# Attention in a fused kernel: reciprocals widened on GpSimd and transposed, last scores in two equal halves, first k loads from ACT's queue, a new table of places

## Chip, cores and metric

The kernel runs on one core of a Trainium2 chip. The metric is the device time of one execution in microseconds. The engines are called PE (TensorE matmul; PEld is its weight load), DVE (VectorE), ACT (ScalarE), POOL (GpSimd) and SP (SyncE, which here issues most DMAs).

## The reference

Three layers follow one another. The change is in the first one alone.

```
# q, k, v: (4 batches, 8 heads, 576 positions, 64), float32
scores = scale * np.matmul(q, k.transpose(0, 1, 3, 2))
mask = block_i >= block_j                    # blocks of 64 positions
scores = np.where(mask, scores, -1000000000.0)
scores = scores - np.max(scores, axis=-1, keepdims=True)
attn = np.exp(scores)
attn = attn / (np.sum(attn, axis=-1, keepdims=True) + 1e-09)
x = np.matmul(attn, v)                       # -> (2304 tokens, 512)
...
h = x @ w_in                                 # 512 -> 2048
g = np.maximum(h, 0.0) + np.log1p(np.exp(-np.abs(h)))
x = g @ w_out                                # 2048 -> 512
...
# routed layer: 8 experts of 512 -> 1024 -> 512, for tokens with x @ w_skip > 0
```

## The kernel before

**Attention.** The 32 heads are worked on in 16 pairs of heads. A pair's 576 queries are four tiles of 128 (t = 0 to 3) and a last one, t = 4 (TAIL), which holds the last 64 queries of both heads side by side in 128 rows. For each pair the kernel runs these steps. In brackets stand the engine and the function; a step's digits are tile and head, so TP40 is step TP of tile 4.

- T (PE, `transposes_qk`): transposes q (T0), k (T1) and the last rows of both (T2); T3 is the first 128 rows of pair 0. H (ACT, `split_high`) and L (DVE, `split_low`) split the result into a high and a low part.
- S (PE, `scores`): the scores of tiles 0 and 1, 2, 3 and 4, three products each (high x high, high x low, low x high). M (DVE, `maxima`) and E (ACT, `exps`): maxima, exponentials and their sums into `sm`.
- TP (PE, `transposes_p`) and EV (ACT or DVE, `evacuate_p`): transposed probabilities, brought out of PSUM. TP40 ends with a fifth transpose (L440) into the bank `v`, which EV5 (DVE) evacuates.
- V (PE, `values`): V00 for the first 256 queries, V10 for the rest.
- R (DVE, `reciprocals`): the nine sums of each row become reciprocals, and each is written as a high and a low part into `rr`. RT (PE, L490) transposes `rr`; RK (ACT, L494) copies the result to `rT`; RM (PE, L501 and L503) multiplies `rT` with the constant `spread`, so that each row of 64 outputs gets its query's reciprocal. RX (ACT) brings that out of PSUM, and N0, N1 (DVE) multiply the values with it.
- C (POOL, DVE, ACT): one piece of the weights of w_in and w_out is converted beside each pair. ldqk, ldv and ldp (SP) load the rows of a later pair and a later piece.

**What sets the order.** Each engine works its instructions off in program order. The steps of neighbouring pairs are mixed: `WHEN` gives each step a place in units of a pair, `SHIFT` corrects it for pairs 0, 1, 2, 14 and 15, and `in_order` emits, of the steps whose needs and buffers are met, the one with the lowest place:

```
step:      steps_of[key] = Step(do, needs, p + WHEN[name] + SHIFT.get((p, name), 0.0))
in_order:  if best is not None and s.when >= best.when:
               continue
```

The tiles in PSUM that T, TP and RM write come from a pool of two (`tp`), so each such step waits for the evacuation of an earlier one. The scores have two buffers (`s`).

**Start and end.** Before the steps, SP issues the loads of pairs 0 and 1 in order (`load_first`, `load_pair`), and PE runs 15 matmuls whose result nobody reads (`keep_busy`). With the last pair's steps are mixed the first splits of x and of weights (L546 to L557) and the first matmuls with w_in (`layer1`, L568, called layer 1 below; `layer2`, L620, called layer 2, multiplies with w_out).

Of the kernel before, what the change touches and what calls it, by code (L numbers as in the profile page):

```python
# [9 lines left out]
F32 = mybir.dt.float32  # L10
# [12 lines left out]
def attention_softplus_moe_kernel(  # L23
# [133 lines left out]
    def load_pair(p, names="qkv", first=0):  # L157

        b, hp = divmod(p, NP)
        for nm in names:  # L160
            src = {"q": q, "k": k, "v": v}[nm]
            t = ld[p, nm] if first else (v_p if nm == "v" else qk_p).tile([P, TT, 2, D], F32, tag=nm, name=nm + "r")
            full = S // P
            for h in range(2):
                nc.sync.dma_start(
                    out=t[:, first:full, h, :],
                    in_=src[b, 2 * hp + h, first * P:full * P, :].rearrange("(t p) d -> p t d", p=P),
                )
            if nm == "q":
                for h in range(2):  # L170
                    r = slice(h * D, (h + 1) * D)
                    nc.sync.dma_start(out=q_last[p % 2][r, r], in_=src[b, 2 * hp + h, full * P:S, :])
            else:
                nc.sync.dma_start(
                    out=t[:, full, :, :], in_=src[b, 2 * hp:2 * hp + 2, S - P:S, :].rearrange("h p d -> p h d")
                )
            ld[p, nm] = t

    def load_first():
        for nm, src in (("q", q), ("k", k)):  # L180
            t = ld[0, nm] = qk_p.tile([P, TT, 2, D], F32, tag=nm, name=nm + "r")
            nc.sync.dma_start(out=t[:, 0, :, :], in_=src[0, 0:2, 0:P, :].rearrange("h p d -> p h d"))
# [104 lines left out]

    NR = 2 * FULL + 1
    spread = pt_p.tile([P, TT + 1, P], F32R, tag="spread", name="spread")
    rrs = [pt_p.tile([P, P], F32R, tag=f"rr{i}", name=f"rr{i}") for i in range(2)]  # L290
# [72 lines left out]
    def scores(p, t):  # L363
# [26 lines left out]
    def maxima(p, t):  # L390

        ps, mx = sc_ps[p, t]
        if t == TAIL:
            nc.vector.tensor_reduce(
                out=mx[:, 0:1], in_=ps.rearrange("p h n -> p (h n)")[:, 0:S], axis=AX.X, op=ALU.max, negate=True
# [91 lines left out]
    rs = {}  # L487
# [676 lines left out]
    nc.scalar.preload_act_table_set("natural_log_exp_and_others")  # L1164
# [3 lines left out]
    load_pair(0, "qk", 1)  # L1168
    load_pair(1, "qk")
# [4 lines left out]
    nc.vector.memset(ones, 1.0)  # L1174
# [13 lines left out]

    def setup_spread():
        for t in range(TT):  # L1190
            for h in range(2):
                c = 2 * t + (h if t < TAIL else 0)
                a, b = (ident[:, x:x + 1].to_broadcast([P, D]) for x in (c, NR + c))
                nc.gpsimd.tensor_tensor(
                    out=spread[:, t + h if t == TAIL else t, h * D:(h + 1) * D], in0=a, in1=b, op=ALU.add
                )
# [6 lines left out]
    class Step:  # L1203
# [20 lines left out]
        "Cc": 0.783, "Cd": 0.485, "Ce": -4.674, "ldp": 1.12, "ldqk": -8.02, "ldv": -4.508, "spread": 0.656,  # L1224
        "setup": 9.277, "load_routing": -1.996, "move": 0.847, "x00": 0.917, "x10": 0.463, "x01": -0.61, "x11": -1.972,
        "x02": -0.686, "x12": -4.773, "x03": -0.39, "x13": 2.078, "wi0": -5.142, "wi1": -0.474, "wi2": 1.753,
        "l10": 3.513, "l11": 15.15, "sp": 16.397,
# [470 lines left out]
```

## Time and profile before

| | us |
|---|---|
| median of 3 runs | 721.88 (721.18 to 723.02) |
| the profiled execution | 721.51 |
| its span | 719.8 |
| PE busy | 688.5 (96%) |
| DVE busy | 473.8 (66%) |
| ACT busy | 369.1 (51%) |
| POOL busy | 155.8 (22%) |

The times of the trace count from the span's start. The shares of the whole span mix the stages; a stage is read by itself from the table of windows. A matmul's row overlaps the next one's, so the time that PE needs for one is read from the distance of two starts. The idle time in front of an instruction is put down to what ended it. The granted clock of 0.989 is a mean over the span.

### The profile page before, as it was taken

To read this page: it belongs to the slowest core of one execution; us is meant where nothing else is said; L and a number is where in the kernel's file an instruction comes from. 1 tells how busy PE (TensorE), PEld (TensorE's weight loads), DVE (VectorE), ACT (ScalarE), POOL (GpSimd) and SP (SyncE) were. 2 spreads that over 40 slices of the span, in tenths; PEclk is the share of its full clock that TensorE was granted. 3 is DMA by queue.
4 is the path that set the end of the run, shared out by engine and by line. 5 is a ranking of instruction groups with operands and counts; after the bars stand their busy time and mean duration, and the time that the engine had idled before them with its cause. 6 is when DMAs were issued, how large, how long until landed. Compare 5 with 4: busy or idle time off the path is not lost. (4 is left out here: it accounts for less than half of the span.)

```text
span 719.8 us, 11563 instructions
## 1 busy us (share of the span) xinstructions
PE 688.5 (96%) x4184; PEld 534.6 (74%) x4184; DVE 473.8 (66%) x983; ACT 369.1 (51%) x884; POOL 155.8 (22%) x177
## 2 busy tenths in 40 slices
PE   6999999999979999999999999999999999987996
PEld 5767777777757888888888888888888777776742
DVE  4677777868786985668665688767665355564322
ACT  3877887878776655465444454444453232320111
POOL 1311112121244543112211122112110021113120
PEclk9999999999999999999999999999999999998999
DMA  6534435542210011011101011100002030984620
GB/s 155 133 85 95 109 89 108 123 115 69 52 59 30 31 58 30 30 59 60 30 29 59 29 48 41 58 30 31 0 1 86 32 118 11 337 303 165 225 76 11
DMA packets 88740, 57.80 MB, mean 80 GB/s; under 512 B 67391, under 2 KB 76607, under 8 KB 88674
## 3 DMA queue, kind: packets, MB, share of 16 engines
q1 hardware_dynamic: 87378, 54.73, 26.1%
q0 software_dynamic: 1296, 2.24, 1.0%
q8 instruction: 35, 0.57, 0.3%
q14 instruction: 31, 0.25, 0.1%
HBM read 46.16 MB, written 10.92 MB: 79 GB/s over the span
## 5 line engine op out<-in xcount | busy, mean ns | idle before, releaser
L568 PE MATMUL h<-xs,wi 128*128 128x512 f32 (+1 forms) x960 | 217.4, 376 | 0.0
L568 PEld LDWEIGHTS h<-xs,wi 128*128 128x128 f32 x960 | 170.5, 191 | 35.9 <-issue 0.9
L620 PE MATMUL o<-wo,gh 128*128 128x512 f32 x576 | 182.6, 398 | 0.0
L620 PEld LDWEIGHTS o<-wo,gh 128*128 128x128 f32 x576 | 106.3, 188 | 23.3
L267 POOL TENSOR_TENSOR cc<-cc,cb 128x512 f32<-128x512 f32 (+1 forms) x40 | 43.5, 1087 | 355.9 <-DVE cb L265 164.6
L583 DVE SCALAR_TENSOR_TENSOR e<-h,e 128x512 f32<-128x512 f32 (+1 forms) x80 | 50.8, 635 | 104.7 <-ACT e L581 104.2
L620 PE MATMUL o<-wo,gl 128*128 128x512 f32 x288 | 114.1, 396 | 0.0
L579 ACT ACTIVATE e<-h 128x512 f32<-128x512 f32 (+1 forms) x80 | 44.1, 551 | 134.3 <-PE h L568 134.3
L409 ACT ACTIVATE p<-s,mx 128x128 f32<-128x128 f32 (+2 forms) x144 | 78.4, 552 | 8.1 <-DVE mx L399 5.7
L589 DVE TENSOR_TENSOR gl<-e,gh 128x512 fp32r<-128x512 f32 (+1 forms) x80 | 65.4, 818 | 6.5
L399 DVE TENSOR_REDUCE mx<-s 128x2 f32<-128x256 f32 (+1 forms) x64 | 52.5, 822 | 19.0 <-PE s L388 9.8
L620 PEld LDWEIGHTS o<-wo,gl 128*128 128x128 f32 x288 | 54.2, 188 | 13.2
L437 PE MATMUL tp<-ident,p 128*128 128x128 f32 x384 | 59.6, 285 | 2.7 <-DMA vr<-in_v_dram 1.0
L463 ACT ACTIVATE pt<-tp 128x512 f32<-128x512 f32 (+1 forms) x80 | 43.8, 553 | 30.9 <-PE tp L437 30.6
L481 PE MATMUL v<-pt,vr 128*64 128x320 f32 (+4 forms) x448 | 50.3, 364 | 0.0
L581 ACT ACTIVATE e<-e 128x512 f32<-128x512 f32 (+1 forms) x80 | 47.2, 590 | 2.5
L580 ACT ACTIVATE e<-e 128x512 f32<-128x512 f32 (+1 forms) x80 | 47.2, 590 | 2.6
L588 DVE CAST gh<-e 128x512 fp32r<-128x512 f32 (+1 forms) x80 | 43.8, 547 | 6.4
L437 PEld LDWEIGHTS tp<-ident,p 128*128 128x128 f32 x384 | 41.8, 142 | 5.9 <-issue 1.3
L751 POOL DMA_INDIRECT lst<-pay,si x18 | 17.7, 984 | 126.8 <-DVE pay L744 83.2
L481 PEld LDWEIGHTS v<-pt,vr 128*64 128x64 f32 x448 | 29.3, 136 | 18.4 <-issue 2.7
L259 ACT ACTIVATE cc<-raw 128x512 f32<-128x512 uint32 (+1 forms) x40 | 22.9, 573 | 24.3 <-POOL ca L268 24.3
(249 smaller groups left out, 945.2 us busy)
## 6 DMA issues: line engine op xcount, KB each, us to landing
xs<-in_moe_w_dram SPq DMA_DIRECT2D x16, 512.0 KB, 8.2
raw<-in_moe_w_in_dram SPq DMA_DIRECT2D x12, 512.0 KB, 3.7
raw<-in_moe_w_out_dram SPq DMA_DIRECT2D x12, 512.0 KB, 3.2
xd<-xT SPq DMA_DIRECT2D x18, 256.0 KB, 4.0
out_dram<-xT SPq DMA_DIRECT2D x18, 256.0 KB, 4.1
vr<-in_v_dram SPq DMA_DIRECT2D x32, 128.0 KB, 2.5
qr<-in_q_dram SPq DMA_DIRECT2D x30, 128.0 KB, 2.8
kr<-in_k_dram SPq DMA_DIRECT2D x30, 128.0 KB, 2.7
```

The lines of the kernel that those rows point to most:

```text
L399: nc.vector.tensor_reduce(out=mx[:, c:c + 2], in_=ps[:, :, columns(t)], axis=AX.X, op=ALU.max, negate=True)
L409: nc.scalar.activation(out=pn[t, h], in_=x, func=AF.Exp, bias=mx[:, c:c + 1], accum_out=sums[p][:, 0, 2 * t + h:2 * t + h + 1])
L437: nc.tensor.transpose(ps[:, at:at + P], pn[t, g][:, j * P:(j + 1) * P], ident)
L463: nc.scalar.activation(out=dst, in_=x, func=AF.Copy)
L481: nc.tensor.matmul(out=ps[h * D:(h + 1) * D, c0 - q0:q1 - q0], lhsT=vt[:, kt, h, :], rhs=rhs, start=(kt == 0), stop=(kt == nk - 1), skip_g ...
L568: nc.tensor.matmul(out=ps[:, 0:n], lhsT=a[:, kc, :], rhs=b[:, 0:n], start=(kc == 0 and j == 0), stop=(kc == KC - 1 and j == 2),)
L579: nc.scalar.activation(out=e[:, 0:n], in_=ps[:, 0:n], func=AF.Abs)
L580: nc.scalar.activation(out=e[:, 0:n], in_=e[:, 0:n], func=AF.Exp, scale=-1.0)
L581: nc.scalar.activation(out=e[:, 0:n], in_=e[:, 0:n], func=AF.Ln, bias=1.0)
L583: nc.vector.scalar_tensor_tensor(out=g[:, 0:n], in0=ps[:, 0:n], scalar=0.0, in1=e[:, 0:n], op0=ALU.max, op1=ALU.add)
L589: nc.vector.tensor_tensor(out=gl[:, 0:n], in0=g[:, 0:n], in1=gh[:, 0:n].bitcast(F32), op=ALU.subtract)
L620: nc.tensor.matmul(out=acc[c, t], lhsT=a[:, ts], rhs=b, start=(fc == f0 and j == 0), stop=(fc == f1 - 1 and j == 2),)
```

## The change

- Reciprocals: `rr`, `rT` and `spread` go, with RT, RK and the two operations that made high and low parts. A new step RB (POOL, L493) copies eight of the nine reciprocals of each row 64 times, to `rb` (128x512). RM becomes five transposes (L502, L504): four of `rb`, and one of the ninth reciprocal, broadcast to 128 columns, into the bank `v`. RX evacuates the last 64 queries in two halves of 64 rows. RM now also needs EV5.
- The last scores are two groups of three matmuls of 288 columns each, in place of 512 and 64.
- The first loads of k (four DMAs) are issued from ACT's queue, ahead of its table load. Six such matmuls of `keep_busy` (idle matmuls, below) are put before each of T0 and T1 of pair 0.
- The table of places is new throughout; the set-up of the routed layer moves to the start.

```
-            for k0, n in ((0, FULL * P), (FULL * P, REM)):
+            n = S // 2
+            for g in range(2):
                 for j, (x, y) in enumerate(((bh, kh), (bh, kl), (bl, kh))):
                     nc.tensor.matmul(
-                        out=ps[:, int(k0 > 0), 0:n], lhsT=x, rhs=y[:, k0:k0 + n],
-                        start=(j == 0), stop=(j == 2),
+                        out=ps[:, g, 0:n], lhsT=x, rhs=y[:, g * n:(g + 1) * n], start=(j == 0), stop=(j == 2),
                     )
...
     def reciprocals(p):
 
-        sm = sums.pop(p)
-        t = rrs[p % 2]
+        sm = sums[p]
         nc.vector.tensor_scalar(out=sm[:, 1, :], in0=sm[:, 0, :], scalar1=1e-9, scalar2=None, op0=ALU.add)
         nc.vector.reciprocal(out=sm[:, 0, :], in_=sm[:, 1, :])
-        nc.vector.tensor_copy(out=t[:, 0:NR], in_=sm[:, 0, :])
-        nc.vector.tensor_tensor(out=t[:, NR:2 * NR], in0=sm[:, 0, :], in1=t[:, 0:NR].bitcast(F32), op=ALU.subtract)
...
-    def rows_of_reciprocals(p):
-        nc.tensor.transpose(pv[p, 0][:, HALF:HALF + P], rrs[p % 2].bitcast(F32), ident)
-
-    def keep_rows(p):
-        rs[p] = st_p.tile([P, P], F32R, tag="rT", name="rT", bufs=2)
-        nc.scalar.activation(out=rs[p], in_=pv[p, 0][:, HALF:HALF + P], func=AF.Copy)
+    def widen_reciprocals(p):
+
+        r = sums[p][:, 0, 0:2 * FULL]
+        rbs[p] = pt_p.tile([P, 2 * FULL, D], F32, tag="rb", name="rb")
+        nc.gpsimd.tensor_copy(
+            out=rbs[p], in_=r.rearrange("p (c o) -> p c o", o=1).to_broadcast([P, 2 * FULL, D])
+        )
 
     def spread_reciprocals(p):
 
         ps = pts[p, "r"] = ps_t.tile([P, 512], F32, tag="tp", name="tp")
-        r = rs.pop(p)
+        rb = rbs.pop(p).rearrange("p c d -> p (c d)")
         for t in range(FULL):
-            nc.tensor.matmul(out=ps[:, t * P:(t + 1) * P], lhsT=spread[:, t, :], rhs=r, start=True, stop=True)
-        for h in range(2):
-            nc.tensor.matmul(
-                out=pv[p, 0][:, HALF:HALF + REM], lhsT=spread[:, TAIL + h, :], rhs=r[:, h * REM:(h + 1) * REM],
-                start=(h == 0), stop=(h == 1), skip_group_check=True,
-            )
+            nc.tensor.transpose(ps[:, t * P:(t + 1) * P], rb[:, t * P:(t + 1) * P], ident)
+        r = sums.pop(p)[:, 0, NR - 1:NR]
+        nc.tensor.transpose(pv[p, 0][:, HALF:HALF + P], r.to_broadcast([P, P]), ident)
...
+            queue = nc.scalar if (nm, first) == ("k", 1) else nc.sync
...
+        if p == 0 and part < 2:
+            keep_busy(6)
...
     WHEN = {
-        "T3": -1.506, "H3": -4.329, "L3": -3.148, "T0": -0.851, "H0": -5.283, "L0": -4.901, "T1": -0.314,
+        "T3": -1.826, "H3": -30.966, "L3": -27.97, "T0": -0.797, "H0": -29.404, "L0": -27.87, "T1": -0.348,
...
-        add("RT", (), rows_of_reciprocals, [k("R"), k("V", 0, 0)], args=())
-        add("RK", (), keep_rows, [k("RT")], args=())
-        add("RM", (), spread_reciprocals, [k("RK"), k("V", 0, 0)], args=())
-        ring("rr", 2, k("R"), [k("RT")])
+        add("RB", (), widen_reciprocals, [k("R")], args=())
+        ring("rb", 1, k("RB"), [k("RM")])
+        ring("sm", 2, k("S", 0), [k("RM")])
+        add("RM", (), spread_reciprocals, [k("RB"), k("EV5"), k("V", 0, 0)], args=())
```

**The order on PE, a pair in the middle, before.** From step T2 (`q_last` and the last rows `kr`) to the second half of the values (`v<-pt`, 64x320). `p_144` is the probabilities of the last tile, `rr_139` the packed reciprocals. Rows that only repeat the one above are left out, here and in the fences below.

```order
L316 MATMUL tp<-ident,q_last_123 128x128 [waits DMAHW5_49,DMAHW4_49,DVE_49]
L316 MATMUL tp<-ident,kr 128x128 [waits DMAHW0_49]
L490 MATMUL v<-ident,rr_139 128x128
L437 MATMUL tp<-ident,p_144 128x128 [waits Activation_49]
L440 MATMUL v<-ident,p_144 128x128 [waits Activation_49]
L384 MATMUL s<-k0h,q0h 128x512 x2
...
L312 MATMUL tp<-ident,kr 128x128 [waits DMAHW7_49,DMAHW6_49,Activation_49]
L501 MATMUL tp<-rT,spread 128x128 [waits DVE_49]
L503 MATMUL v<-rT,spread 128x64 [waits DVE_49]
L481 MATMUL v<-pt_912,vr 64x320 x6
```

The transpose of the reciprocals (L490) stands ahead of step TP40, whose last transpose (L440) writes the same bank `v` and waits for ACT.

The same place after the change, from V00 (64x256) on; `p_141` is now the last tile's probabilities, `p_138` those of tile 3.

```order
L481 MATMUL v<-pt_912,vr 64x256 [waits DMAHW1_49]
L437 MATMUL tp<-ident,p_141 128x128 [waits Activation_49]
L440 MATMUL v<-ident,p_141 128x128
L384 MATMUL s<-k0h,q0h 128x384 x2
...
L316 MATMUL tp<-ident,q_last_123 128x128 [waits DMAHW5_49,DMAHW4_49,DVE_49]
L437 MATMUL tp<-ident,p_138 128x128 [waits Activation_49]
L384 MATMUL s<-k0h,q0h 128x512 [waits Activation_49]
L502 MATMUL tp<-ident,rb 128x128 [waits Activation_49,Pool_49]
L504 MATMUL v<-ident,sm 128x128 [waits DVE_49]
L312 MATMUL tp<-ident,kr 128x128 [waits DMAHW7_49,DMAHW6_49,DVE_49]
L481 MATMUL v<-pt_904,vr 64x320 x6
```

TP40 with L440 has moved ahead of the 384-column scores and of T2; the reciprocals are transposed after the 512-column scores and before T1, and wait for POOL there.

**The order on PE at the end of attention, before.** From the last pair's V00 to the first products of layer 1 (`h<-xs,wi`); `p_144` is the last tile's probabilities.

```order
L481 MATMUL v<-pt_3056,vr 64x128 x2
L437 MATMUL tp<-ident,p_141 128x128 [waits Activation_49]
L437 MATMUL tp<-ident,p_142 128x128 [waits Activation_49]
L490 MATMUL v<-ident,rr_139 128x128 [waits DVE_49]
L437 MATMUL tp<-ident,p_144 128x128 [waits Activation_49]
L440 MATMUL v<-ident,p_144 128x128 [waits Activation_49]
L501 MATMUL tp<-rT,spread 128x128 [waits PE_49]
L568 MATMUL h<-xs,wi 128x512 x2
...
L481 MATMUL v<-pt_3154,vr 64x320 [waits Activation_49]
```

The same place after the change.

```order
L481 MATMUL v<-pt_3035,vr 64x128 x2
L437 MATMUL tp<-ident,p_141 128x128 [waits Activation_49]
L440 MATMUL v<-ident,p_141 128x128
L437 MATMUL tp<-ident,p_138 128x128 [waits Activation_49]
L437 MATMUL tp<-ident,p_139 128x128 [waits Activation_49]
L502 MATMUL tp<-ident,rb 128x128 [waits Activation_49,Pool_49]
L504 MATMUL v<-ident,sm 128x128 [waits DVE_49]
L481 MATMUL v<-pt_3103,vr 64x320
L570 MATMUL h<-xs,wi 128x512 [waits Activation_49]
```

L490 is gone, TP40 has moved to the front, and the last values, which stood behind the first product of layer 1, now stand ahead of it.

**The order on POOL, one pair in the middle, after the change.** `ca`, `cc` and `wi` are the weight conversion's tiles.

```order
L251 TENSOR_TENSOR ca<-raw 128x256 [waits DMAHW4_49,Pool_49]
L493 COPY rb<-sm 128x512 [waits DVE_49,PE_49,Activation_49]
L268 TENSOR_TENSOR cc<-cc,cb 128x256 [waits DVE_49]
L269 TENSOR_TENSOR wi<-ca,cc 128x256 [waits Pool_49]
L251 TENSOR_TENSOR ca<-raw 128x256 [waits DMAHW4_49,Pool_49]
```

The copy is new; it stands between the first and the last part of a piece's conversion.

## Rows read from the trace of the kernel before

**Rows 1.** Table of stages: us, busy us (instructions) per engine, granted clock, DMA share, GB/s.

```profile
0.00:8.57 8.57, 4.59 (x25) 3.31 (x26) 1.49 (x6) 2.54 (x5) 2.87 (x16) 1.00 0.46 105
8.57:22.04 13.47, 11.54 (x63) 9.29 (x62) 8.86 (x18) 7.18 (x26) 2.72 (x6) 1.00 0.81 189
22.04:47.82 25.78, 24.20 (x215) 18.51 (x214) 18.83 (x44) 20.11 (x63) 5.41 (x14) 1.00 0.43 103
47.82:197.51 149.69, 147.52 (x1298) 112.53 (x1297) 115.14 (x278) 119.67 (x372) 26.48 (x45) 1.00 0.40 95
197.51:229.02 31.51, 26.61 (x183) 20.27 (x182) 22.05 (x41) 21.16 (x52) 13.52 (x11) 0.95 0.14 42
229.02:555.00 325.98, 325.98 (x1474) 266.55 (x1473) 231.72 (x367) 162.93 (x288) 78.32 (x60) 1.00 0.11 37
```

**Rows 2.** PE in order of time, one pair: start, us, instruction, count.

```profile
74.69 0.44 PE L384 MATMUL s<-k1h,q1h 64*128 64x384 f32 x2
74.98 0.34 PE L384 MATMUL s<-k1l,q1h 64*128 64x384 f32 x2
75.15 0.34 PE L384 MATMUL s<-k1h,q1l 64*128 64x384 f32 x2
...
76.93 0.33 PE L316 MATMUL tp<-ident,q_last 128*128 128x128 f32 x1
...
77.21 0.27 PE L490 MATMUL v<-ident,rr 128*128 128x128 f32 x1
77.31 0.60 PE L437 MATMUL tp<-ident,p 128*128 128x128 f32 x4
78.06 0.33 PE L440 MATMUL v<-ident,p 128*128 128x128 f32 x1
...
79.12 0.20 PE L388 MATMUL s<-ones,unseen 64*128 64x64 bf16 x2
...
80.43 2.28 PE L481 MATMUL v<-pt,vr 128*64 128x320 f32 x20
...
83.16 0.47 PE L373 MATMUL s<-k1h,bd1h 128*128 128x512 f32 x1
...
84.18 1.09 PE L437 MATMUL tp<-ident,p 128*128 128x128 f32 x8
85.20 0.33 PE L384 MATMUL s<-k0h,q0h 64*128 64x128 f32 x2
```

**Rows 3.** PE's weight loads, the same pair: who waited for whom, us, times, longest.

```profile
PEld v L440 <- ACT rT L494: 0.4, 1, 0.4
PEld tp L316 <- DVE q0l L340: 0.3, 1, 0.3
```

**Rows 4.** The start in order of time, all engines.

```profile
0.82 1.28 ACT L1164 ACT_TABLE_LOAD   x1 [0.82 <-PEq L1682]
...
4.12 1.12 SPq L165 DMA_DIRECT2D kr<-in_k_dram  x2
...
4.72 0.87 PE L312 MATMUL tp<-ident,qr 128*128 128x128 f32 x3 [0.46 <-DMA qr<-in_q_dram]
...
7.34 0.88 PE L312 MATMUL tp<-ident,kr 128*128 128x128 f32 x3 [1.75 <-DMA kr<-in_k_dram]
...
18.71 1.06 PE L437 MATMUL tp<-ident,p 128*128 128x128 f32 x4
```

**Rows 5.** PE's longest waits from 197.51 to 218 us.

```profile
PE v L490 <- DVE rr L420: 3.2, 1, 3.2
PE v L490 <- DVE pt L466: 1.1, 1, 1.1
```

**Rows 6.** PE in order of time, the first products of layer 1.

```profile
217.15 4.03 PE L568 MATMUL h<-xs,wi 128*128 128x512 f32 x12
...
223.31 5.86 PE L568 MATMUL h<-xs,wi 128*128 128x512 f32 x24
```

**Rows 7.** POOL's groups of instructions by form: busy us, mean ns, idle before.

```profile
L549 POOL TENSOR_TENSOR xs<-xT,xs 128x512 fp32r<-128x512 f32 x10 | 14.4, 1446 | 12.6 <-ACT xs L546 10.6 <-DVE xs L548 2.0
```

More of the change, by code (lines that the diff above doesn't have):

```diff
@@ L164, in load_pair @@
             for h in range(2):
-                nc.sync.dma_start(
+                queue.dma_start(
                     out=t[:, first:full, h, :],
@@ L171, in load_pair @@
                     r = slice(h * D, (h + 1) * D)
-                    nc.sync.dma_start(out=q_last[p % 2][r, r], in_=src[b, 2 * hp + h, full * P:S, :])
+                    queue.dma_start(out=q_last[p % 2][r, r], in_=src[b, 2 * hp + h, full * P:S, :])
             else:
-                nc.sync.dma_start(
+                queue.dma_start(
                     out=t[:, full, :, :], in_=src[b, 2 * hp:2 * hp + 2, S - P:S, :].rearrange("h p d -> p h d")
@@ L179, in load_first @@
     def load_first():
-        for nm, src in (("q", q), ("k", k)):
+        for nm, src, queue in (("q", q, nc.sync), ("k", k, nc.scalar)):
             t = ld[0, nm] = qk_p.tile([P, TT, 2, D], F32, tag=nm, name=nm + "r")
-            nc.sync.dma_start(out=t[:, 0, :, :], in_=src[0, 0:2, 0:P, :].rearrange("h p d -> p h d"))
+            queue.dma_start(out=t[:, 0, :, :], in_=src[0, 0:2, 0:P, :].rearrange("h p d -> p h d"))
     w_in_i = w_in.bitcast(I32)
@@ L288, in attention_softplus_moe_kernel @@
     NR = 2 * FULL + 1
-    spread = pt_p.tile([P, TT + 1, P], F32R, tag="spread", name="spread")
-    rrs = [pt_p.tile([P, P], F32R, tag=f"rr{i}", name=f"rr{i}") for i in range(2)]
     pt2 = pt_p.tile([P, 2, REM], F32, tag="pt2", name="pt2")
@@ L394, in maxima @@
             nc.vector.tensor_reduce(
-                out=mx[:, 0:1], in_=ps.rearrange("p h n -> p (h n)")[:, 0:S], axis=AX.X, op=ALU.max, negate=True
+                out=mx[:, 0:1], in_=ps[:, :, 0:S // 2], axis=AX.XY, op=ALU.max, negate=True
             )
@@ L406, in exps @@
             sums[p] = st_p.tile([P, 2, NR], F32, tag="sm", name="sm", bufs=2)
-        x = ps.rearrange("p h n -> p (h n)")[:, 0:S] if t == TAIL else ps[:, h, columns(t)]
+        if t == TAIL:
+            x, y = ps[:, :, 0:S // 2], pn[t, h].rearrange("p (g n) -> p g n", g=2)
+        else:
+            x, y = ps[:, h, columns(t)], pn[t, h]
         c = 2 * int(t == 1) + h
         nc.scalar.activation(
-            out=pn[t, h], in_=x, func=AF.Exp, bias=mx[:, c:c + 1], accum_out=sums[p][:, 0, 2 * t + h:2 * t + h + 1]
+            out=y, in_=x, func=AF.Exp, bias=mx[:, c:c + 1], accum_out=sums[p][:, 0, 2 * t + h:2 * t + h + 1]
         )
     def reciprocals(p):
-        sm = sums.pop(p)
-        t = rrs[p % 2]
+        sm = sums[p]
         nc.vector.tensor_scalar(out=sm[:, 1, :], in0=sm[:, 0, :], scalar1=1e-9, scalar2=None, op0=ALU.add)
         nc.vector.reciprocal(out=sm[:, 0, :], in_=sm[:, 1, :])
-        nc.vector.tensor_copy(out=t[:, 0:NR], in_=sm[:, 0, :])
-        nc.vector.tensor_tensor(out=t[:, NR:2 * NR], in0=sm[:, 0, :], in1=t[:, 0:NR].bitcast(F32), op=ALU.subtract)
     PT = {}
@@ L485, in values @@
                 )
[L487 to L494 removed]
+    rbs = {}
+    def widen_reciprocals(p):
[4 more added lines that the diff above has]
+        )
     def spread_reciprocals(p):
         ps = pts[p, "r"] = ps_t.tile([P, 512], F32, tag="tp", name="tp")
[L499 removed]
+        rb = rbs.pop(p).rearrange("p c d -> p (c d)")
         for t in range(FULL):
[L501 to L506 removed]
+            nc.tensor.transpose(ps[:, t * P:(t + 1) * P], rb[:, t * P:(t + 1) * P], ident)
+        r = sums.pop(p)[:, 0, NR - 1:NR]
+        nc.tensor.transpose(pv[p, 0][:, HALF:HALF + P], r.to_broadcast([P, P]), ident)
     def x_of(p, q0, q1):
@@ L514, in keep_reciprocals @@
         nc.scalar.activation(out=x_of(p, 0, FULL * P), in_=pts.pop((p, "r")), func=AF.Copy)
-        nc.scalar.activation(out=x_of(p, FULL * P, S), in_=pv[p, 0][:, HALF:HALF + REM], func=AF.Copy)
+        for h in range(2):
+            r = slice(h * D, (h + 1) * D)
+            nc.scalar.activation(
+                out=x_of(p, FULL * P, S)[r], in_=pv[p, 0][r, HALF + h * REM:HALF + (h + 1) * REM], func=AF.Copy
+            )
     def normalise(p, half):
@@ L1163, in attention_softplus_moe_kernel @@
     ctx.enter_context(tc.manual_schedule())
-    nc.scalar.preload_act_table_set("natural_log_exp_and_others")
+    nc.vector.memset(ones, 1.0)
     for i in range(2):
@@ L1168, in attention_softplus_moe_kernel @@
     load_pair(0, "qk", 1)
+    nc.scalar.preload_act_table_set("natural_log_exp_and_others")
     load_pair(1, "qk")
@@ L1173, in attention_softplus_moe_kernel @@
     load_pair(1, "v")
-    nc.vector.memset(ones, 1.0)
     keep_busy(15)
@@ L1179, in attention_softplus_moe_kernel @@
         nc.gpsimd.memset(unseen[h * D:h * D + 1, 0:BLK], UNSEEN)
-    for i in range(2):
-        nc.gpsimd.memset(rrs[i].bitcast(F32), 0.0)
     nc.gpsimd.memset(pt2[0:P - REM], 0.0)
-    nc.gpsimd.memset(spread.bitcast(F32), 0.0)
     nc.gpsimd.memset(zeros, 0.0)
@@ L1187, in attention_softplus_moe_kernel @@
     nc.gpsimd.memset(blank[:, :, :, 1], 0)
[L1189 to L1196, printed above, removed]
     X0 = "avvpavvp"
@@ L1215, in attention_softplus_moe_kernel @@
     WHEN = {
[8 rows of a table removed]
[L1224 to L1227, printed above, removed]
[8 rows of a table added]
+        "Cd": 1.473, "Ce": -0.906, "ldp": 0.848, "ldqk": -26.137, "ldv": 0.17, "setup": -0.563, "load_routing": 5.725,
+        "move": -0.595, "x00": 1.495, "x10": 2.034, "x01": -3.314, "x11": 0.114, "x02": 0.457, "x12": 1.475,
+        "x03": 0.222, "x13": -0.717, "wi0": 0.166, "wi1": -26.631, "wi2": 1.078, "l10": 6.37, "l11": 7.064,
+        "sp": 0.291,
     }
     SHIFT = {
[40 rows of a table removed]
-        (0, "setup"): -0.494, (0, "load_routing"): -0.944, (15, "move"): -0.122, (15, "x00"): 0.015, (15, "x01"): -0.8,
-        (15, "x02"): -0.002, (15, "x12"): -0.023, (15, "x03"): -0.172, (15, "x13"): -0.299, (15, "wi0"): -0.377,
-        (15, "wi1"): 0.868, (15, "wi2"): 0.077, (15, "l10"): 1.051, (15, "l11"): -0.144, (15, "sp"): -1.119,
[28 rows of a table added]
+        (2, "Ce"): -0.385, (2, "ldp"): 0.487, (15, "ldqk"): 0.167, (15, "ldv"): 0.687, (15, "L0"): 0.288,
[8 rows of a table added]
+        (15, "Cd"): -2.47, (15, "Ce"): 0.189, (15, "ldp"): 1.597, (0, "setup"): 0.607, (0, "load_routing"): -1.46,
[3 rows of a table added]
     }
@@ L1417, in attention_softplus_moe_kernel @@
     ]
-    step(("spread", 0), setup_spread)
-    steps_of["RM", 0].needs.append(("spread", 0))
     step(("setup", 0), setup_routing)
```

93 rows, old and new, of tables (SHIFT, WHEN) are left out of this document.

## Prediction

> **What bounds the kernel now.** The table of stages comes first [rows 1]. From 229 us to 555 us TensorE (PE) is busy in every microsecond; the change edits nothing there, so that stretch and what follows it only slide to the left or the right. The change lives in the attention stage, 0 to 229 us. Its middle, 47.82 to 197.51 us, holds 12 pairs of heads at 149.69 / 12 = 12.47 us each; PE is busy for 147.52 of 149.69 us, VectorE (DVE) for 115.14, ScalarE (ACT) for 119.67. So PE sets the pace of a pair, and ACT and DVE have about a fifth of the time left. Around that middle lie three stretches where PE does not run full: the start up to the first scores of pair 1 (22.04 us), the two pairs after it (25.78 us, 12.89 each, against 12.47 later), and the tail from the last pair's first scores to the first matmul of layer 2 (31.51 us, PE busy 26.61).
>
> Next comes PE's order of time through one pair [rows 2] and its waits there [rows 3]. The reader should see that matmul groups stand nose to tail, that a transpose (fp32, 128x128) follows another after 0.10 to 0.11 us (77.21 to 77.31), and that one hole is left: four transposes start at 77.31, the fifth (L440) could follow at 77.31 + 4 x 0.11 = 77.75 and starts at 78.06. L440 waits for ACT's copy rT; that is 0.31 us of PE in every pair.
>
> The start [rows 4] shows one queue, SP's, issuing all loads: k's remaining rows are issued from 4.12 us on, and the transposes of k start at 7.34 us, though those of q were done at 4.72 + 0.87. It also shows PE at its lower level: four transposes take 1.06 us at 18.71 against 0.60 us at 77.31. The granted clock is printed as 1.00 for 8.57 to 22.04 us, but rows of that length are those of 1.2 GHz, not 2.4; PE had idled before most groups till then.
>
> The tail [rows 5] shows PE waiting 3.2 us and 1.1 us in front of L490, the transpose of the packed reciprocals (step RT). After the long wait 12 matmuls take 4.03 us, where 24 of the same later take 5.86 [rows 6].
>
> **The middle, per pair.**
> - RT goes: one transpose, 0.11 us (76.93 to 77.31, three transposes in 0.38 us) [rows 2].
> - ACT's copy rT (step RK) goes, and L440's wait of 0.31 us with it [rows 2, 3]. L440 now stands right behind the four transposes of its own step and waits for nothing of its own. The gap to the next group (78.06 to 78.32, 0.26 us) becomes the 0.20 us that follows a row of transposes elsewhere: eight start at 84.18, the last at 85.00 (0.16 + 6 x 0.11 later), the next group at 85.20. That is 0.06 us more.
> - From the end of one score group (79.12) to the second half of the values (80.43) there are 1.31 us with four transposes of k and six reciprocal matmuls. Now there are nine transposes: 0.13 + 0.16 + 7 x 0.11 + 0.20 = 1.26 us. Gain 0.05 us. So the new way to widen the reciprocals is hardly cheaper on PE itself; it is the round trip through ACT that is saved.
> - Last scores: three matmuls of 512 columns and three of 64 take 83.16 to 84.18, 1.02 us. 384-column matmuls are 0.17 us apart (74.98 to 75.15), and the first of a group costs 0.12 us extra (74.69 to 74.98). In proportion 288 columns take 0.128 us, so 6 x 0.128 + 0.12 = 0.89. Gain 0.13 us; if small matmuls were as slow as 512-column ones it would be nothing.
> - Step T2 waited for DVE's split, its weight load by 0.3 us [rows 3]; now the values, TP40 and the 384-column scores stand between. I take 0.13 us for what the matmul itself lost; bounds 0 and 0.3.
>
> The sum is 0.11 + 0.31 + 0.06 + 0.05 + 0.13 + 0.13 = 0.79, taken as 0.80 us per pair, to 11.67. Is there cover for what is added? ACT loses a 128x128 copy and gains one 64x64 copy: nothing. ACT has 119.67 / 12 = 9.97 us of work in 11.67, DVE at most 9.60 (it also loses two short operations): both still fit. GpSimd's new copy of 128x512 was never run here. The nearest rows from above are two-input operations of that size, 1.45 us [rows 7]; from below it is nothing. I take 1.0 us. It starts after the second maximum of a pair and is wanted only behind the 512-column scores; even from the 384-column scores to the end of the 512-column ones the old order takes 4.4 us (74.69 to 79.12) [rows 2]. The conversions queued behind it on GpSimd have no hurry, since PE does not need their weights before the tail. So 12 x 0.80 = 9.6 us, with bounds of 0.45 and 0.90 per pair: 5.4 to 10.8.
>
> **The start.** k's three DMAs leave ACT's queue from about 1.3 us on, instead of 4.12 on SP's [rows 4]. The transposes of k then wait for q's, at about 5.6 us with the six idle matmuls in front, instead of 7.34: 1.7 us. The table load (1.28 us at 0.82 us) now stands behind four issues; two issues take 1.12 us, so it ends near 4.3 us, about when ACT's first copy is due: nothing lost. What is late next is DVE's split of k. The twelve added idle matmuls fill PE's holes ahead of the first scores, so the higher level may come before 21 us. Of the 13.47 us to pair 1 PE is busy for 11.54 at the low level and DVE for 8.86 [rows 1]: with PE fast the stretch cannot fall under 8.86, so this is worth 0 to 4.6 us. I take 1.8, nearer the lower end because ACT's exponentials then set the pace. Start: 3.5 us, bounds 1.0 and 5.5.
>
> A rule bears on this. DMA packets kept the 16 engines 46% busy in the first 8.57 us and 81% in the next 13.47 [rows 1]. The Trainium skill (Trainium Kernel Development and Optimization, Key Constraints) says that DMAs of all issuing queues share the same 16 DMA engines, and a second queue saves only its issue time. By the row of 46% there is still room early, so the issue time is worth having and the term stays 1.7 us; were the engines full, as the 81% row says of later, it would be nothing. That is a rival below.
>
> **The two pairs after it.** 25.78 us against 2 x 11.67 = 23.3 us: 2.4 us; I take 2.2, bounds 0.9 and 2.6.
>
> **The tail.** RT, the instruction that waited 3.2 + 1.1 us [rows 5], is gone, and the reciprocals of the last pair (R) are moved ahead of DVE's splits. The half-speed stretch that followed cost 4.03 - 5.86 / 2 = 1.1 us [rows 6]. That is 5.4 us. But the last GpSimd copy is queued behind two conversions, and the reciprocal transposes and the last values now stand ahead of layer 1 and wait for that copy and for DVE's last evacuation. I take 5.0 us, bounds 2.5 and 6.1.
>
> **Sum.** 9.6 + 3.5 + 2.2 + 5.0 = 20.3 us. The profiled execution took 721.51 us (span 719.8), 0.37 below the median of 721.88. So 721.51 - 20.3 = 701.2, and 701.5 for a median. All low bounds give 721.5 - 9.8 = 712, all high ones 721.5 - 25.0 = 696.5.
>
> **Rivals.**
> - *A new wait takes the old one's place* (0.21). ACT now runs the last exponential of a pair ahead of the evacuation on which T0 of the next waits; both are due in PE's last microsecond of a pair. If PE loses there what it lost at L440, 0.31 us per pair, the middle gives 12 x 0.31 = 3.7 us back: 705.2. For it: ACT would be 85% busy. Against: ACT idles for a fifth now, and the exponential is ready before the evacuation.
> - *The clock rises no sooner than before* (0.16): 1.8 us less, 703.3.
> - *The DMA engines are the limit early* (0.06), the rule's case: 1.7 us less, 703.2.
> - *The tail's wait returns as one for the last GpSimd copy* (0.10): 3.2 us less, 704.7.
> - *The reorder gives back what the edits win*, so the change does not do what it says (0.02): 721.5.
> - *Slower* (0.05): GpSimd delivers late in every pair. Each pair has one copy, and PE's in-order queue stands behind it with k's transposes, the values and all later scores. The copy has some 4.4 us of cover. To eat the other gains it must make PE wait 20.3 / 15 = 1.35 us in each of 15 pairs, so end 5.8 us or more after the reciprocals; at 7 us the total is 721.5 - 20.3 + 15 x 2.6 = 740. Against: two-input operations of its size take 1.45 us.
>
> **Chances and range.** My case has 0.40. A measurement of this kernel can tell about 0.3%, 2 us, from no change. All cases but the last two lie over 2 us below 721.9: faster 0.92, the same 0.02, slower 0.06 (the 0.05 and a remainder for something unseen). Several of the smaller rivals together with low bounds reach 709; the high side of my case reaches 697. Range 697 to 709.
>
> **What would show it.** Right: pairs of 11.6 to 11.8 us in the middle; no wait at L440; six 288-column matmuls in 0.9 us; GpSimd's copy at 0.5 to 1.5 us with no PE wait on it; k's transposes before 6 us; no PE idle over 1 us in the tail. Wrong: PE waiting for GpSimd ahead of the reciprocal transposes, or for ACT ahead of q's transposes; pairs of 12 us or more; transposes still over 1 us for four at 18 us; a half-speed stretch before layer 1.

## Result and profile after

The changed kernel takes 716.03 us (median of 6 runs, 712.65 to 717.06), the kernel before beside it 721.53 (6 runs, 720.31 to 723.02): ratio 0.991, 95% interval 0.989 to 0.994. It is faster, by 0.9% instead of the forecast 2.8%; 701.5 and the range 697 to 709 were missed. The profiled execution took 716.66 us, its span 714.9, granted clock 0.992.

The table of stages of the changed kernel (stretch; us, busy us and instructions of PE, PEld, DVE, ACT, POOL; granted clock, DMA share, GB/s), cut at the same events as [rows 1]:

```profile
0.00:7.69 7.69, 5.74 (x37) 4.53 (x37) 1.49 (x6) 2.69 (x5) 2.79 (x20) 1.00 0.58 129
7.69:19.70 12.01, 10.46 (x65) 8.32 (x64) 8.48 (x27) 7.01 (x26) 1.22 (x2) 1.00 0.84 195
19.70:43.95 24.25, 22.93 (x210) 17.56 (x209) 19.10 (x42) 19.86 (x62) 5.35 (x8) 1.00 0.47 112
43.95:196.15 152.20, 143.81 (x1273) 107.44 (x1272) 118.71 (x241) 120.56 (x372) 32.22 (x48) 1.00 0.40 94
196.15:222.34 26.19, 24.92 (x178) 18.26 (x178) 22.79 (x38) 20.03 (x51) 17.20 (x15) 1.00 0.15 42
```

Against [rows 1]: start 22.04 - 19.70 = 2.3 us won, the two next pairs 1.5, the tail 31.51 - 26.19 = 5.3; but the middle, where 9.6 us should have come from, is **2.5 us longer** (152.20 against 149.69), though PE is busy for 3.7 us less. The rest, from layer 2 to the end, took 1.8 us more. Sum 2.3 + 1.5 - 2.5 + 5.3 - 1.8 = 4.8 us; the profiled executions are 721.51 - 716.66 = 4.85 apart.

PE in order of time, one pair of the middle of the changed kernel (start, us, instruction, count, idle before and its releaser):

```profile
97.11 0.87 PE L481 MATMUL v<-pt,vr 128*64 128x256 f32 x8
98.62 0.66 PE L437 MATMUL tp<-ident,p 128*128 128x128 f32 x4 [0.64 <-ACT pt L463]
99.11 0.27 PE L440 MATMUL v<-ident,p 128*128 128x128 f32 x1
99.31 0.44 PE L384 MATMUL s<-k1h,q1h 64*128 64x384 f32 x2
...
101.83 0.66 PE L502 MATMUL tp<-ident,rb 128*128 128x128 f32 x4
...
102.96 2.28 PE L481 MATMUL v<-pt,vr 128*64 128x320 f32 x20
105.16 0.98 PE L437 MATMUL tp<-ident,p 128*128 128x128 f32 x5
105.90 0.38 PE L374 MATMUL s<-k1h,bd1h 128*128 128x288 f32 x1
...
106.78 1.04 PE L437 MATMUL tp<-ident,p 128*128 128x128 f32 x8
107.75 0.33 PE L384 MATMUL s<-k0h,q0h 64*128 64x128 f32 x2
```

The edits do what they were to do: L440 follows its four transposes at once, the six 288-column matmuls take 106.78 - 105.90 = 0.88 us, RM waits for nobody. But the eight matmuls of the first values, 0.88 us in the kernel before (76.05 to 76.93), now hold 97.11 to 98.62 because step TP40 waits 0.64 us for ACT's evacuation EV21, which empties the tile of `tp` that TP40 writes; and the five transposes at 105.16 hold 0.74 us instead of 0.52, for step L1 on DVE, which empties another. Those two new waits are 0.85 us per pair.

What ACT, DVE and POOL do there, the same pair (one view per engine):

```profile
97.38 0.37 ACT L412 ACTIVATE p<-s,mx 128x128 f32<-128x128 f32 x1 [0.91 <-DVE sm L419]
97.74 0.36 ACT L412 ACTIVATE p<-s,mx 128x128 f32<-128x128 f32 x1
98.08 0.49 ACT L463 ACTIVATE pt<-tp 128x384 f32<-128x384 f32 x1
```

```profile
96.24 1.02 DVE L399 TENSOR_REDUCE mx<-s 128x2 f32<-128x256 f32 x2 [0.52 <-PE s L388]
...
103.18 0.72 DVE L253 TENSOR_SCALAR cb<-raw 128x256 int32<-128x256 int32 x1
103.94 0.78 DVE L256 SCALAR_TENSOR_TENSOR cb<-raw,cb 128x256 int32<-128x256 int32 x1
...
104.98 0.67 DVE L344 TENSOR_TENSOR k0l<-tp,k0h 128x512 fp32r<-128x512 f32 x1
```

```profile
102.22 0.73 POOL L268 TENSOR_TENSOR cc<-cc,cb 128x256 f32<-128x256 f32 x1 [3.86 <-DVE cb L266]
103.02 0.73 POOL L269 TENSOR_TENSOR wo<-ca,cc 128x256 f32<-128x256 f32 x1
103.83 0.61 POOL L251 TENSOR_TENSOR ca<-raw 128x256 f32<-128x256 f32 x1
```

The first exponential (E01, 97.38) starts 0.12 us after *both* first maxima of the pair (M0 and M1, 96.24 to 97.26); the row names L419, but that operation is not what it reads. Behind it E00 stands ahead of EV21 on ACT. In the table of before the order was M0, E01, M1 and E01, EV21; DVE, then ACT of that kernel:

```profile
86.31 0.42 DVE L399 TENSOR_REDUCE mx<-s 128x2 f32<-128x256 f32 x1 [0.58 <-PE s L388]
87.26 0.69 DVE L399 TENSOR_REDUCE mx<-s 128x2 f32<-128x512 f32 x1 [0.53 <-ACT p L409]
```

```profile
86.77 0.37 ACT L409 ACTIVATE p<-s,mx 128x128 f32<-128x128 f32 x1
87.13 0.48 ACT L463 ACTIVATE pt<-tp 128x384 f32<-128x384 f32 x1
```

And DVE's two operations of step Cb run beside POOL, the first beside the second operation of step Ce (L269), the second beside the step Ca behind it (L251): in the kernel before they took 282 and 425 ns (means of twelve), now 720 and 794.

So the theory after the result: the edits are worth what was forecast, and the new table of places gives it back through these two waits. Rivals: the edits themselves are worth little; the lost time is elsewhere and would only move.

### The profile page after: what moved, and what is told of

Read it like the earlier page. It is cut to its first block, busy times and chain, and to the rows that moved or that the text cites. A ratio compares the mean times of both kernels' runs of the same rounds, so it can differ in the third digit from the quotient of the medians.

```text
span 714.9 us, 11536 instructions
## 1 busy us (share of the span) xinstructions
PE 681.4 (95%) x4164; PEld 525.9 (74%) x4164; DVE 478.7 (67%) x951; ACT 369.1 (52%) x884; POOL 163.7 (23%) x180
## 5 line engine op out<-in xcount | busy, mean ns | idle before, releaser
L570 PEld LDWEIGHTS h<-xs,wi 128*128 128x128 f32 x960 | 168.6, 188 | 36.7 <-issue 0.8
L268 POOL TENSOR_TENSOR cc<-cc,cb 128x512 f32<-128x512 f32 (+1 forms) x40 | 43.4, 1086 | 262.0 <-DVE cb L266 191.5
L437 PE MATMUL tp<-ident,p 128*128 128x128 f32 x384 | 61.2, 284 | 12.1 <-ACT pt L463 9.1
L399 DVE TENSOR_REDUCE mx<-s 128x2 f32<-128x256 f32 (+1 forms) x64 | 50.9, 819 | 10.3 <-PE s L388 9.1
```

The lines of the kernel that those rows point to most:

```text
L399: nc.vector.tensor_reduce(out=mx[:, c:c + 2], in_=ps[:, :, columns(t)], axis=AX.X, op=ALU.max, negate=True)
L437: nc.tensor.transpose(ps[:, at:at + P], pn[t, g][:, j * P:(j + 1) * P], ident)
L570: nc.tensor.matmul(out=ps[:, 0:n], lhsT=a[:, kc, :], rhs=b[:, 0:n], start=(kc == 0 and j == 0), stop=(kc == KC - 1 and j == 2),)
```

## Experiments

All twelve kernels ran beside the kernel before, whose median was 722.2 to 722.3 us in each of the three series. "A pair" is the distance from one pair's first scores to the next one's in the steady middle: 12.43 us before, 12.63 changed.

**The old table with the new code.** `WHEN` and `SHIFT` are those of before, without the entries of the steps that are gone; in `WHEN` the entries that differ are (cut out of their lines):

```
-        "RT": 1.517, "RK": -1.952, "spread": 0.656,
+        "RB": 1.096,
```

> All edits of the change (GpSimd's copy, transposed reciprocals, equal halves, loads of k from ACT's queue, idle matmuls), but with the table of places of before; RB gets a place right behind R, RM keeps its own. Theory (the edits save on PE what was forecast and the new table gives it back): a pair in the middle takes 11.65 to 11.9 us (12.43 less 0.66 by the steps of PE that the changed kernel's trace shows, bounds 0.5 and 0.8), with no wait in front of L440 and none on GpSimd; the middle's twelve pairs take about 141 us; the kernel 703 to 711 us, depending on the tail. Rival (the edits themselves are worth nothing in the order of before, because RM now waits for GpSimd or for EV5): pairs of 12.3 us or more, the kernel at 716 to 720.

Measured: 707.59 us (ratio 0.980, 0.978 to 0.981), a pair 11.63 us, and PE without a hole. Stages from pair 3 on, then PE in one pair, then PE's waits from 184.5 to 216 us:

```profile
44.05:184.50 140.45, 140.13 (x1276) 107.75 (x1275) 110.64 (x254) 119.53 (x372) 33.37 (x57) 1.00 0.44 101
184.50:216.01 31.51, 26.47 (x179) 19.42 (x179) 22.02 (x37) 21.36 (x52) 15.68 (x14) 0.95 0.16 45
```

```profile
83.39 0.60 PE L437 MATMUL tp<-ident,p 128*128 128x128 f32 x4
83.83 0.27 PE L440 MATMUL v<-ident,p 128*128 128x128 f32 x1
84.03 0.50 PE L384 MATMUL s<-k0h,q0h 64*128 64x512 f32 x2
```

```profile
PE tp L502 <- POOL rb L493: 3.1, 1, 3.1
```

The theory holds: 12.43 - 11.63 = 0.80 us per pair, the forecast's sum. The new table costs 12.63 - 11.63 = 1.00 us in each pair. The tail shows the other side: with the old table it is as long as before (31.51 us), because the wait of 3.2 us in [rows 5] comes back as one of 3.1 us for GpSimd's copy. The tail's gain belongs to the new table.

**Why E01 waits.** First a tile of its own for M1's result:

```
-            sc_ps[p, 1] = sc_ps[p, 0]
+            sc_ps[p, 1] = sc_ps[p, 0][0], st_p.tile([P, 4], F32, tag="mx1", name="mx1")
```

> Changed kernel, but the negated maxima of tile 1 get a tile of their own, so that ACT's first exponential of a pair (E01) waits for the first maximum alone, not for both. Theory (two new waits, the larger one made by the shared tile of maxima): E01 starts some 0.55 us sooner in a pair, the evacuation EV21 behind it too, the 0.63 us that PE loses in front of the transposes TP40 fall to 0.1 or less, a pair in the middle takes 12.05 to 12.15 us instead of 12.63, the kernel 708 to 710 us where the changed one takes 716. Rival (the order on ACT alone makes the wait, E00 in front of EV21): E01 starts no sooner and a pair stays at 12.63. Rival (the lost time only moves to the next wait): TP40's wait goes but a pair stays above 12.4.

Measured: 715.63 us, a pair 12.63. The theory of the shared tile of maxima falls. Next, the places of E01 and M1 exchanged in pairs 3 to 14 (`"M1": -29.0`), with the shared tile:

> Changed kernel, but in pairs 3 to 14 the maximum M1 is emitted behind the exponential E01, as in the table of before; nothing else moves. Theory (E01 waits for both maxima because, with nothing emitted between the two on DVE and no reader in between, DVE signals only after the second; a tile of its own for M1 could not change that): E01 starts 0.45 to 0.6 us sooner, EV21 too, PE's 0.63 us in front of TP40 fall to 0.15 or less, M1 starts only after E01 has read the shared tile, a pair takes 12.05 to 12.2 us, the kernel 709 to 711 us. Rival (E01 waits for something else that ends when M1 does, such as the scores' buffer or the sums): pair 12.63. Rival (M1 now late makes R, L0 or E00 late in turn): wait at TP40 gone, pair above 12.3.

Measured: a pair 12.88 us, slower (a single run, 719.31). E01 does start sooner, 0.52 us behind M0's start instead of 1.14, but now the wait sits behind it. ACT's waits in one pair of that run, then PE's:

```profile
ACT p L412 <- DVE mx L399: 1.0, 2, 0.8
```

```profile
PE tp L437 <- ACT pt L463: 0.9, 1, 0.9
```

M1 starts when E01 has ended, E00 when M1 has ended, and EV21 stands behind E00: TP40 waits 0.9 us. M1 waits for E01 even where it has a tile of its own for its result, in run e7 (told below):

```profile
94.18 0.69 DVE L399 TENSOR_REDUCE mx<-s 128x2 f32<-128x512 f32 x1 [0.58 <-ACT p L412]
```

What is left in common is the tile of scores in PSUM, which M1, E01 and E00 only read. To test that, M1 gets its own tile for the result, as in run e1, and reads a constant tile instead (the maxima of tile 1 are left out), in the order of the changed kernel:

```
+        elif t == 1:
+            nc.vector.tensor_reduce(
+                out=mx, in_=ident.rearrange("p (o n) -> p o n", o=1).to_broadcast([P, 4, P]), axis=AX.X, op=ALU.max,
+                negate=True
```

> The kernel of run e1 (tile of its own for the maxima of tile 1), but M1 reduces as many elements of a constant tile in SBUF instead of the scores of tile 1, which are left out of the maxima (the exponentials of tile 1 then have a constant offset). The order on every engine is that of the changed kernel. Theory (E01 waits for M1 because both read one tile of scores in PSUM, on two engines, and such readers run in program order): E01 starts 0.45 to 0.6 us sooner, PE's 0.63 us in front of TP40 fall to 0.15 or less, a pair takes 12.0 to 12.15 us. Rival (DVE's signal for M0 is given only with M1's because M1 follows at once): E01 still waits for M1, a pair stays at 12.63.

Measured: a pair 12.01 us (a single run, 702.51), and no PE wait in front of TP40. DVE, then ACT of that run:

```profile
90.07 0.42 DVE L404 TENSOR_REDUCE mx<-s 128x2 f32<-128x256 f32 x1 [0.53 <-PE s L388]
90.41 0.67 DVE L398 TENSOR_REDUCE mx<-ident 128x4 f32<-128x512 f32 x1
```

```profile
90.59 0.37 ACT L417 ACTIVATE p<-s,mx 128x128 f32<-128x128 f32 x1 [0.29 <-DVE mx L404]
```

E01 runs beside M1 as soon as M1 reads elsewhere; that is worth 12.63 - 12.01 = 0.62 us per pair. M1 still follows M0 at once, so the rival that DVE signals M0 only with M1 falls; and the operation that the row of the changed kernel names (L419, L424 in this run) stands behind M1 here too, at 91.00 us, after E01's start. So two engines that read one tile of scores are put one behind the other, in program order. Whether it is the tile that counts or one of its two banks, no run separates. The Trainium skill (PSUM — Partial Sum Buffer, PSUM bank collisions raise a hardware error) says that two engines may not touch the same part of one bank of PSUM at once, reads against reads included, and that the program must guard the bank. The trace agrees: in the changed kernel E01 starts 0.12 us after M1's end, and in run e10 beside M1.

**The order on ACT.** In pairs 3 to 14 E00 behind EV21 and H0 (`"E00": 0.2055`):

> Changed kernel, but in pairs 3 to 14 the exponential E00 is emitted behind EV21 and H0 on ACT, as it was in the table of before; the maxima still share a tile. Theory: EV21 and H0 start 0.35 us sooner (one 128x128 exponential), PE's wait in front of TP40 falls from 0.63 to about 0.28 us, a pair takes 12.27 us, the kernel about 712 us. Rival (the shared tile of maxima is the whole cause): no change, 12.63. Rival (E00 now delays E11, EV40 and H2): a pair above 12.4 with a new wait in front of the 384-column scores or of T2.

Measured: 712.41 us (0.986, 0.984 to 0.989), a pair 12.33 us, TP40's wait 0.3 us. The theory holds: an exponential of 0.36 us in front of EV21 was worth 12.63 - 12.33 = 0.30.

**GpSimd beside DVE.** In pairs 3 to 14 step Cd, and with it POOL's Ce, behind L1 (`"Cd": 1.7`):

> Changed kernel, but in pairs 3 to 14 step Cd (two operations of DVE) is emitted behind L1, so that GpSimd's two two-input operations Ce, which follow it, no longer run beside DVE's step Cb. Theory (DVE is late with L1 because GpSimd's operations slow Cb): the two operations of Cb take about 0.28 and 0.44 us instead of 0.72 and 0.78, L1 starts some 0.6 us sooner, PE's 0.22 us in front of TP00 go, a pair takes about 12.4 us, the kernel 713 to 714 us. Rival (Cb's length has nothing to do with GpSimd): Cb stays at 1.5 us, L1 and the pair as they were, 12.63. Rival (Ce now slows EV00 or M4 in place of Cb): L1 sooner, but a new wait at V00, TP10 or S0, a pair at 12.5 or more.

Measured: 714.27 us, a pair 12.40. DVE, then POOL of that run:

```profile
102.16 0.28 DVE L253 TENSOR_SCALAR cb<-raw 128x256 int32<-128x256 int32 x1
102.47 0.42 DVE L256 SCALAR_TENSOR_TENSOR cb<-raw,cb 128x256 int32<-128x256 int32 x1
```

```profile
104.67 0.74 POOL L268 TENSOR_TENSOR cc<-cc,cb 128x256 f32<-128x256 f32 x1 [7.24 <-DVE cb L266]
```

The theory holds: apart from POOL's operations Cb is as short as before, and TP00's wait is gone. The Trainium skill (SBUF — State Buffer, Who interferes with whom) says that GpSimd and some VectorE operations share one pair of ports and that the later one then waits. The trace of the changed kernel agrees: in each of the twelve pairs of the middle L253 starts 0.16 to 0.17 us later than an operation of POOL's step Ce (L269, once L268) and ends 0.15 to 0.16 us after it.

**All three repairs** in pairs 3 to 14 (M1 behind E01 with a tile of its own, E00 and Cd as above), then the same in pairs 1 to 14:

> Changed kernel with three repairs in pairs 3 to 14, the rest of the new table as it is: M1 behind E01 with a tile of its own, E00 behind EV21 and H0, Cd behind L1. Theory (the two waits, 0.63 us in front of TP40 and 0.22 us in front of TP00, are all that the new order of a pair costs): both go, a pair takes 11.75 to 11.9 us, the kernel 704 to 707 us. Rival (with these gone other waits come up at once, the new order is tight in more than two places): pairs of 12.0 us or more, above 708.

> The three repairs of run e7 (M1 behind E01 with a tile of its own, E00 behind EV21 and H0, Cd behind L1) in pairs 1 to 14 instead of 3 to 14. Theory (the pairs around the start lose to the same two waits): the windows that started with the scores of pairs 2 and 3 take 11.7 to 12.0 us instead of 12.41 and 12.57, the later ones 11.69 as in run e7, the kernel 702 to 703 us. Rival (these windows are slow for reasons of the start: DMA, the clock): no gain over run e7's 703.7.

Measured: 703.66 us (0.973, 0.969 to 0.978), a pair 11.69, no PE wait in a pair; and 705.11 us (0.977, 0.974 to 0.981; 702 to 703 was expected), the two earlier windows 11.75 and 11.69 instead of 12.41 and 12.57. Both beat both kernels. The second wins what was expected in those windows (its middle lasts 140.30 us, that of the first 141.20), but from layer 2 to the end the first took 490.7 us and the second 492.9; that stretch, which the table does not touch, scatters by more than the gain, and the intervals overlap.

**Old places for pairs 2 to 13 alone**, the new ones for start and tail:

> Changed kernel with the places of before for the steps of pairs 2 to 13 (loads of q and k excepted; RB right behind R), and the new places for the start, pairs 0, 1, 14 and 15, the set-up of the routed layer and the tail. Theory (the new table loses 1.0 us in each pair of the middle, but wins in start and tail): pairs of 11.63 us between the fifth and the thirteenth, no 12.4 us pair where the set-up of the routed layer stood, the tail as in the changed kernel (26.2 us from the last pair's first scores to layer 2), so 11 x 1.0 less than the changed kernel: 703 to 706 us. Rival (a pair of 11.63 us needs the whole old table, the seams cost what is won): above 709. Rival (the tail of the changed kernel was short only because its middle was slow and GpSimd's and DVE's conversions had time): the tail at 29 us or more, 707 to 709.

Measured: 708.98 us (0.982, 0.979 to 0.985). Pairs of 11.63 us and a short tail (26.84 us, counted to the second matmul of layer 2, where the changed kernel has 26.92), but two seams: windows of 15.62 and 13.20 us, where the changed kernel has 12.41 and 12.63. The rival of the seams had the cause, at the edge of its range (above 709); the rival of the tail was wrong.

**The start.** The loads of k back on SP's queue (`queue = nc.sync`), and without the idle matmuls (`keep_busy(6)` removed):

> Changed kernel, but the four first loads of k are issued from SP's queue, in the order of before. Theory (these loads brought the first scores forward): the transposes of k start at 7.0 to 7.4 us instead of 6.33, the first scores at 8.4 to 8.8 us instead of 7.69 (8.57 before), the first scores of pair 1 0.5 to 1 us later than the 18.8 to 20.1 us of the runs so far, the middle's pairs unchanged at 12.63. Rival (the two queues share the DMA engines, k arrives no sooner either way): first scores at 7.6 to 7.8 us.

> Changed kernel without the twelve idle matmuls ahead of T0 and T1 of pair 0. Theory of the prediction (they bring the higher clock sooner): the first scores start at about 7.1 us instead of 7.69 since nothing stands ahead of T1, but the granted clock rises near 21 us as before instead of 17, pair 1's first scores start at 20.3 to 21 us instead of 19.70, the kernel 0.5 to 1.5 us slower. Rival (the earlier rise comes from the loads of k and the new order alone): rise still near 17 us, pair 1 at 19.1 us, the kernel 0.6 us faster.

Measured, a single run each (717.93 and 716.48 us): with k on SP its transposes start at 7.45 us, the first scores at 8.69 and those of pair 1 at 20.72; the changed kernel has 6.33, 7.69 and 19.70. PE in the changed kernel, then with k on SP:

```profile
5.03 0.87 PE L312 MATMUL tp<-ident,qr 128*128 128x128 f32 x3 [0.64 <-DMA qr<-in_q_dram]
5.69 0.85 PE L353 MATMUL busy<-ones 128*128 128x128 bf16 x6
6.33 0.85 PE L312 MATMUL tp<-ident,kr 128*128 128x128 f32 x3
```

```profile
7.45 0.87 PE L312 MATMUL tp<-ident,kr 128*128 128x128 f32 x3 [1.31 <-DMA kr<-in_k_dram]
```

So the loads bring 1.0 us up to the first scores, which start between 7.05 and 7.97 us in all runs with these loads on ACT's queue and between 8.57 and 8.69 in the three without. Without the idle matmuls k is transposed at 5.86, but the next step then waits for DVE's split of q: first scores at 7.86, pair 1 at 19.50. PE in that run:

```profile
5.86 0.84 PE L310 MATMUL tp<-ident,kr 128*128 128x128 f32 x3
7.24 0.48 PE L314 MATMUL tp<-ident,q_last 128*128 128x128 f32 x1 [0.54 <-DVE q0l L338]
...
16.00 1.06 PE L310 MATMUL tp<-ident,kr 128*128 128x128 f32 x4
16.86 0.58 PE L435 MATMUL tp<-ident,p 128*128 128x128 f32 x3
```

The upper level comes between 16.00 and 16.86, in the changed kernel between 16.30 and 17.10 (four transposes 0.96 us, then three 0.54). The theory on the loads held. That on the idle matmuls did not: the rise that it expected near 21 us without them came by 17. One run against one cannot show a small effect of theirs, since the starts of like kernels differ by as much (last section).

**Equal halves alone**, in the kernel before:

> Kernel before with one part of the change alone: the last scores as two groups of three 288-column matmuls. Theory (the forecast's 0.13 us per pair, PE being the bound): the six matmuls take 0.88 instead of 1.02 us and a pair of the middle 12.28 to 12.31 us instead of 12.43, the kernel 2 us less. Rival (something else ends the pair, the saved time becomes a wait): six matmuls 0.88 us, pair 12.40 to 12.43. Rival (small matmuls cost as much as large ones): no change.

Measured: a pair 12.21 us (a single run, 718.76), a gain of 0.22 us, more than expected: the six matmuls 0.15 us less, the eight transposes behind them 0.96 instead of 1.02 us. Its start is that of the kernel before but for the last scores, yet the transposes of k that take 1.06 us there (four at 17.86 us) run at the upper level:

```profile
17.75 0.60 PE L312 MATMUL tp<-ident,kr 128*128 128x128 f32 x4
```

and pair 1 starts at 20.73 us instead of 22.04. In run e10, whose M1 differs in all pairs, four transposes of q take 0.60 us at 11.67 us already (1.06 us at 12.54 in the changed kernel), and pair 1 starts at 17.26.

## Why the prediction was wrong

- **RT, rT, L440, RM, halves (0.80 us per pair): right.** 0.80 us with the old table. By term: RT's 0.11; L440's wait and gap 0.36 (forecast 0.37); the halves 0.15 (0.13), and 0.06 in the transposes behind them, which were not forecast; the nine transposes 0.04 (0.05). For T2's 0.13 there were 0.08, and not for the reason given: T2 stands in its old place in that run, but DVE's split in front of it comes 0.93 instead of 1.35 us behind M1's start, without the two short operations of R. That the sum meets the forecast is in part luck: the 0.06 stand in for what T2 lacks.
- **ACT and DVE "both still fit": the step that failed.** The cover was counted as totals per pair, ACT's 9.97 and DVE's 9.60 us in 11.67, and the order alone was taken to cost nothing. ACT did idle for a fifth, but 0.91 us of that now lies in front of E01, where a chain to PE hangs on it: M0, M1, E01, E00, EV21, TP40. With 0.64 + 0.22 us of waits and small shifts the table costs 1.00 us per pair, 12 us in the middle, of the 15.5 us by which the profiled execution missed 701.2. The rival "the reorder gives back what the edits win" came true in the middle; it had a chance of 0.02 and named no wait, and start and tail kept their gains. The rival "a new wait takes the old one's place" had the right engine and the right kind of mechanism (an exponential put ahead of an evacuation), but another step of PE and a third of the price.
- **GpSimd:** the copy takes 0.61 us (forecast 1.0) and PE never waits for it in the middle. That the conversions behind it "have no hurry" was true for PE's need of their results and missed what they do to DVE while they run: 0.22 us per pair.
- **The start (3.5 us):** 2.3 us; the loads of k gave 1.0 instead of 1.7. Their transposes were forecast for 5.6 us and start at 6.33: they stand behind the idle matmuls, which hold PE from 5.69 to 6.33 and for which 4.72 + 0.87 = 5.6 left no time, and q's transposes in front of these start at 5.03 instead of 4.72. Without the idle matmuls the split of q is late next. The 1.8 us for the clock are not shown to be the change's: without the idle matmuls the rise comes no later, and run e11, with the start of before, had 1.3 us of them. The rule that DMAs of all queues share their engines, which the Trainium skill (Trainium Kernel Development and Optimization, Key Constraints) has, left the term at the issue time; the trace agrees, with the engines busy for 0.58 of the first 7.69 us and k sooner by 1.0 us.
- **The two next pairs (2.2):** 1.5 us. The second of them suffers the same two waits: its window is 12.41 us, and 11.75 in run e12; that of the first hardly moves there (11.84 and 11.90).
- **The tail (5.0 us): right in size**, 5.3 us to the first matmul of layer 2; to the second, which waits in the changed kernel, 31.73 - 26.92 = 4.8. The order is the one given as the reason: the last pair's R starts at 206.05 us, ahead of DVE's splits of x at 206.43. No run moved R alone. With the old table the rival was true to 0.1 us.
- **After layer 2:** taken as sliding only. From the second matmul of layer 2 on it took 491.9 us against 490.5 before. In the twelve runs, which do not differ there on purpose, it lay between 488.9 and 492.9, and at 492.0 in run e11 with the table of before. So the difference is within the scatter, and no run sought its cause.

What stays open: the 0.06 us per pair by which the repaired new order is still behind the old one, and what decides when the clock rises in the start.

## What to carry to other kernels

Free time of an engine is no cover: follow, in the new order, each chain from the first result of a stage to the next thing that PE waits for, and count what stands ahead on every engine of that chain. In PSUM, also count two readers of one tile on two engines as one queue, and give the shorter way to PE the first place. Where edits and a new order come together, run the edits in the old order once; it split this change into 0.80 us won and 1.00 us lost per pair.

## What the runs showed of the hardware

- Run e6, which moved one maximum behind an exponential, lost 0.25 us per pair: M1 waits for E01 there and E00 for M1, three readers of one PSUM tile on two engines in turn (the tile of maxima is shared in that run too).
- A 128x256 operation of DVE went from 282 to 720 ns beside GpSimd's two-input operation of 0.73 us, and one with two inputs from 425 to 794 beside one of 0.61 us (once of 0.73). The first ended 0.15 to 0.16 us after GpSimd's operation in each of twelve pairs, the second 0.28.
- The rise of the granted clock in the start scatters. Runs e2, e4 and e6 have the changed kernel's code up to pair 3; the four transposes of k near 16 us take 1.06 us (lower level) in e2, 0.70 in e4 and 0.60 (upper level) in e6, and pair 1 starts at 19.77, 19.46 and 18.94 us. The upper level can also be lost again: in run e1 it was there at 7.07 us, and three transposes at 14.62 us took 0.90 us, as at the lower one. With the start of before pair 1 started at 22.04 and, in run e11, at 20.73. A single profile of a start is no measure of an edit of that size.
